# One join fewer on VectorE and score groups at places of their own, in a fused attention, Fourier and feed-forward kernel

## The chip, the cores and the metric

One Trainium2 chip, of which the kernel uses one core. The metric is the device time of one execution in microseconds; the time before is the median of three runs. Engines are named as the profile names them: PE (TensorE matmul), PEld (TensorE weight load), DVE (VectorE), ACT (ScalarE), POOL (GpSimd), SP (SyncE, which issues most DMAs).

## The reference, cut to what matters

```python
# q, k, v: (8, 8, 576, 64) float32; moe_w_ch1 (512, 2048) and moe_w_ch2 (2048, 512) float64
scores = q @ k.transpose(0, 1, 3, 2) / 8 - slopes[:, None, None] * abs(rel)   # per head
scores = where((rel >= 0) & (rel < 128), scores, -1e9)
attn = softmax(scores, axis=-1)
x = (attn @ v).transpose(0, 2, 1, 3).reshape(8, 576, 512)
u = x + real(fft(fft(x, axis=1), axis=2))
un = layer_norm(u)                       # no gain, no bias
out = u + relu(un @ w_ch1) @ w_ch2
```

## The kernel before, in words

The kernel works batch by batch (eight batches `b`), and inside a batch by pairs of heads: `p` counts pairs through the whole program, four to a batch. Every step is a small Python function that is put into a heap with a due time (`put(t, f, ...)`); the heap is emptied in order of the due times, and a step may put followers a little later (`after`). That sets the order in which instructions are written down. A planner then orders the instructions of each engine, from that order as a priority and from its own costs of instructions, and each engine runs its list in order. So a due time moves an instruction roughly, and the planner decides the last detail.

A pair `p` begins at `begin_of(p)`, every 6 units of due time from `p = 4` on (before that every 2.2). Its scores are made in three groups, `scores(p, i)` with i = 0, 1, 2, over the query tiles (1, 0), (3, 2) and (4). For each of the two heads a group's matmuls (line 378) fill a PSUM tile `sp`; VectorE then adds the bias and takes the row minimum in one instruction (line 391, written as `P` and `nb`), ScalarE takes the exponential. For batches from `NF = 2` on, products are made from pairs of fp16 parts: `halves` (line 404 and a VectorE instruction) splits the weights of attention, and `flip` (line 413) transposes them by DMA from the SP queue into `pt`. `values` (lines 445 to 447) multiplies `pt` with V into `pv`. For batches 0 and 1 the same is done in float32 with transposes on TensorE (`turn`, lines 422 and 426).

In the first four pairs, `busy` (line 299) adds three matmuls of 512 columns on constant data after each block of matmuls, 180 in all; their results are not used.

After a batch's four pairs come a Fourier transform (`fourier`), the normalisation (`norm`) and the feed-forward part (`ffn`, lines 699 and 713), which is by far the largest part of TensorE's work, spread in small steps over the due times of the following batch.

The float64 weights are read at the start as 32-bit words, two per value, in 16 chunks for each of two matrices, at due times 0 to 8 and 9 to 18.6. For a chunk, `load` brings 512 KB; `rebias` (line 183, ScalarE) takes the upper word as a float32, makes its absolute value and shifts its exponent by a factor of 2^-112; `join` (lines 188 to 190, VectorE) shifts the result left by three bits, joins the top bits of the lower word, and joins the sign bit of the upper word. `gram` (line 198) squares the chunk on TensorE for a scale, and when all 16 are there `high` and `low` (lines 216 and 219) split the scaled matrix into two fp16 parts, which the feed-forward part reads.

For each batch from 2 on, `batch_scales` also reads q, k and v once more through two small slots (lines 253 and 257), for a scale.

The last loop of the kernel puts the pairs' steps; the line that the change touches there is

```python
        for i in range(3):
            put(t + 2 * i * f + (0 if b < NF + 1 else 1 - 2 * ((3 * p + i) % 2)), scores, p, i)
```

With groups numbered 3p + i, group n stands at 2n units. For batches 3 to 7 the term adds one unit to even numbers and takes one from odd ones, so two groups at a time are due at the same place, every four units. `values` for x = 0 to 5 (head of the pair x // 3, tiles of group x % 3) are due at t + x + 5.66 and don't move.

Of the kernel before, what the change touches and what calls it, by code (L numbers as in the profile page):

```python
# [10 lines left out]
F32 = mybir.dt.float32  # L11
# [3 lines left out]
AF = mybir.ActivationFunctionType  # L15
ALU = mybir.AluOpType
# [6 lines left out]
NF = 2  # L23
# [32 lines left out]
def begin_of(p):  # L56
    return 6 * PACE[0] * p if p < 4 else T1 + 6 * (p - 4)
# [6 lines left out]
def forward_of(b):  # L64
    return transform_of(b) + (START - DFT if b else 11 * PACE[1])
# [11 lines left out]
def attn_fft_ffn_kernel(  # L77
# [16 lines left out]
    V, A, G, T = nc.vector, nc.scalar, nc.gpsimd, nc.tensor  # L94
# [46 lines left out]
    def total(m):  # L141
        sums = ps_d.tile([128, 512], F32, name="pd")[:, 0:m.shape[1]]
        T.matmul(sums, misc[:, 7:8].broadcast_to([128, 128]), m, start=True, stop=True)
        return sums

    def root_inv(dst, src):
        V.tensor_scalar(dst, src, 0.5, 2.0 ** -81, ALU.mult, ALU.max)
        V.tensor_scalar(dst.bitcast(I32), dst.bitcast(I32), 1, 0x3F800000, ALU.logical_shift_right, ALU.bitwise_and)
        V.reciprocal(dst, dst)
# [4 lines left out]
    def put(t, f, *a):  # L154
        heappush(queue, (t, next(order), f, a))
# [8 lines left out]
    def weights(wi, t0, dt, t1, dt1):  # L164
        w, top = ((w1, 2.0 ** 7), (w2, 2.0 ** 14))[wi]
        raws, box = {}, {}
        if wi == 0:
            stages = [hbuf[:, o:o + 1024] for o in range(0, 4096, 1024)]
        else:
            stages = [stage[:, 0:1024], stage[:, 1024:2048], wall[1][:, 0]]  # L170
        ns = len(stages)

        def load(c):
            raws[c] = stages[c % ns]
            nc.sync.dma_start(out=raws[c].bitcast(I32), in_=w[:, c * 512:(c + 1) * 512].bitcast(I32))

        def words(c):
            return (raws[c].bitcast(I32).rearrange("p (a b) -> p a b", b=2),
                    wall[wi][:, 1 + c // 2, c % 2 * 512:c % 2 * 512 + 512])

        def rebias(c):
            raw, dst = words(c)
            A.activation(dst, raw[:, :, 1].bitcast(F32), AF.Abs, scale=2.0 ** -112)

        def join(c):
            raw, dst = words(c)
            bits = dst.bitcast(I32)
            V.tensor_scalar(bits, bits, 3, None, ALU.logical_shift_left)
            V.scalar_tensor_tensor(bits, raw[:, :, 0], 29, bits, ALU.logical_shift_right, ALU.bitwise_or)
            V.scalar_tensor_tensor(bits, raw[:, :, 1], -0x80000000, bits, ALU.bitwise_and, ALU.bitwise_or)  # L190

        def gram(c):
            if c == 0:
                box["gram"] = ps_f.tile([128, 512], F32, name="fp")[:, 0:128]
            upper = words(c)[1].bitcast(BF16).rearrange("p (x e) -> p x e", e=2)[:, :, 1]
            for j in range(4):
                blk = upper[:, j * 128:(j + 1) * 128]
                T.matmul(box["gram"], blk, blk, start=(c == 0 and j == 0), stop=(c == 15 and j == 3))

        def top_of():  # L200
            m1 = small.tile([128, 2], F32, name="wm1", tag="m2")
            V.tensor_reduce(m1[:, 0:1], box["gram"], AX.X, ALU.max)
            box["sums"] = total(m1[:, 0:1])

        s = wsc[:, wi:wi + 1]

        def scale():
            root_inv(s, box["sums"])
            V.tensor_scalar_mul(s, s, top * 2.0 ** -64)
            if wi == 1:  # L210
                V.tensor_tensor(wone, wsc[:, 0:1], wsc[:, 1:2], ALU.mult)
                V.tensor_scalar_mul(wone, wone, 8.0)
                V.reciprocal(wone, wone)

        def high(g):
            A.activation(wf[wi][:, g, 0], wall[wi][:, g + 1], AF.Copy, scale=s)  # L216

        def low(g):
            V.scalar_tensor_tensor(wf[wi][:, g, 1], wall[wi][:, g + 1], s, wf[wi][:, g, 0], ALU.mult, ALU.subtract)

        for c in range(16):
            t = t0 + dt * c
            put(-3 + 0.1 * c if c < ns else t + dt * (1 - ns) - 0.05, load, c)
            put(t, rebias, c)
            put(t + dt - 0.1, join, c)
            put(t + 2 * dt - 0.3, gram, c)
        t = t0 + 17 * dt
        put(t, top_of)
        put(t + 0.3, scale)
        for g in range(8):  # L230
            put(t1 + dt1 * g, high, g)
            put(t1 + dt1 * (g + 0.8), low, g)
# [490 lines left out]
    for p in range(4 * B):  # L723
        b, j = divmod(p, 4)
        t, f = begin_of(p), 1 if b else PACE[0]
        put(t - 7 * f if p else -3.2, load, p)
        if b < NF:
            put(t - 3.8 * f if p else -2, convert, p, 0)
            put(t - 1.2 * f, load_v, p)
            put(t + 4.2 * f, v_max, p)  # L730
        else:
            early = p < 4 * NF + 2
            put(t - (1.3 if early else 6.8), load_v, p)
            for what, x in enumerate((4.6, 3.6, -2 if early else 1.2)):
                put(t - x, convert, p, what)
        for i in range(3):
            put(t + 2 * i * f + (0 if b < NF + 1 else 1 - 2 * ((3 * p + i) % 2)), scores, p, i)
            for e in range(2 if b < NF else 0):
                put(t + (2 * i + e + LB + 0.33) * f, turn, p, i, e)
        for x in range(6):  # L740
            put(t + (x + LC + 0.66) * f, values, p, x % 3, x // 3)
        if b < NF and j == 3:
            put(t + 5 * f, f32_scale, b)
# [5 lines left out]
    for b in range(B):  # L749
        t = begin_of(4 * b)  # L750
# [4 lines left out]
        t = forward_of(b)  # L755
# [88 lines left out]
def program(q, k, v, moe_w_ch1, moe_w_ch2):  # L844
    import numpy as np
    import concourse.bacc as bacc

    B = q.shape[0]
    qa = np.ascontiguousarray(q.transpose(0, 1, 3, 2)[..., query_order()]).reshape(B, 4, 128, NQ)
    ka = np.concatenate([k, k[:, :, :NK - S]], axis=2).transpose(0, 1, 3, 2)  # L850
    ka = np.ascontiguousarray(ka).reshape(B, 4, 128, NK)
    idx = np.array([[min(s + p, S - 1) for s in VSTART] for p in range(128)])
    va = np.ascontiguousarray(v[:, :, idx])
    nf = min(B, NF)
    v0 = np.ones((nf, H, 128, 5, 65), np.float32)
    v0[..., 0:D] = va[:nf]
    w1 = np.ascontiguousarray(moe_w_ch1.reshape(4, 128, 16, 128).transpose(1, 2, 0, 3).reshape(128, -1))
    w2 = np.ascontiguousarray(moe_w_ch2.reshape(16, 128, DM).transpose(1, 0, 2).reshape(128, -1))
    w1, w2 = w1.view(np.int64), w2.view(np.int64)
    rel, slope, tab1, tab2 = tables()  # L860
    nc = bacc.Bacc("TRN2", target_bir_lowering=False, num_devices=1, dynamic_dma_scratch_size=1024)
    arrays, args = {}, []
    for name, a in (("q", qa), ("k", ka), ("v", va), ("v0", v0), ("w1", w1), ("w2", w2), ("rel", rel),
                    ("slope", slope), ("tab1", tab1), ("tab2", tab2)):
        arrays[name + "_dram"] = a
        args.append(nc.dram_tensor(name + "_dram", a.shape, mybir.dt.from_np(a.dtype), kind="ExternalInput").ap())
    rows = B * S
    args.append(nc.dram_tensor("out_dram", (rows, DM), F32, kind="ExternalOutput").ap())
    with tile.TileContext(nc, schedule_with_timeline_sim=True) as tc:
        attn_fft_ffn_kernel(tc, *args)  # L870
    return nc, arrays, B
```

## Time and profile before

| | |
|---|---|
| median of 3 runs | 1132.4 us |
| lowest and highest run | 1125.85, 1135.44 us |
| profiled execution, first to last instruction | 1129.0 us |
| mean granted TensorE clock in it | 0.974 |
| TensorE busy (matmul) | 1064.1 us, 94% |
| VectorE busy | 710.9 us, 63% |
| ScalarE busy | 583.7 us, 52% |

The profiled execution is one of its own; its time is its span, 1129.0 us, with whatever lies outside the first and the last instruction not shown. It is 3.4 us under the median of the runs. The busy shares are means over stages with different limits: the first 110 us hold the weights and the first batch's attention, up to some 340 us only the first batch's feed-forward part can fill TensorE, from there to 930 us attention, Fourier and feed-forward parts of following batches run side by side, and after 930 us only feed-forward work is left.

### The profile page before, as it was taken

Reading aid. Unit: us, or ns where it says so; the run is one execution under the profiler, and the core shown is the slowest. Engines: PE = TensorE matmul, PEld = TensorE weight load, DVE = VectorE, ACT = ScalarE, POOL = GpSimd, SP = SyncE. Lnnn points to the kernel's source line nnn. Section 1 sums busy time; section 2 is a strip of 40 time slices with the busy share of each in tenths; the row PEclk is TensorE's granted clock in tenths of the full one; section 3 lists DMA queues with packets and bytes.
Section 4 is the critical chain, followed back from the end, with each engine's and each line's share of the span. In section 5 each row is a group of like instructions: output and inputs, shape, how many; then the busy total and the mean of one; then the engine's idle time right before and its main releaser. Section 6 shows DMA issues by size and latency. Waiting matters only on the chain.

```text
span 1129.0 us, 23955 instructions
## 1 busy us (share of the span) xinstructions
PE 1064.1 (94%) x9296; PEld 742.2 (66%) x9296; DVE 710.9 (63%) x2081; ACT 583.7 (52%) x1380; POOL 19.6 (2%) x59
## 2 busy tenths in 40 slices
PE   7999989978789989999999989999899989999998
PEld 4667767464475757777667667585758567667665
DVE  6989668725866576768677585869575754362111
ACT  5757889657774465437554474456434631151010
POOL 0000000000000000000000000000000000010000
PEclk9999859999799999999999989999999999999999
DMA  9951647666863335332734243333531240010000
GB/s 368 333 156 41 180 129 189 177 160 163 200 138 106 68 96 110 77 89 65 136 93 86 42 116 75 83 87 85 119 91 32 41 106 1 20 43 24 19 10 20
DMA packets 191506, 117.82 MB, mean 104 GB/s; under 512 B 154400, under 2 KB 164128, under 8 KB 191392
## 3 DMA queue, kind: packets, MB, share of 16 engines
q1 hardware_dynamic: 190816, 114.84, 40.6%
q8 instruction: 73, 1.20, 0.4%
q10 hardware_dynamic: 576, 1.45, 0.3%
q14 instruction: 41, 0.34, 0.1%
HBM read 70.63 MB, written 9.44 MB: 71 GB/s over the span
## 4 chain that ended last, share of the span: by engine, by line
PE 63%; DVE 13%; DMA 10%; ACT 9%; issue 3%; SPq 1%; POOL 0%; DVEq 0%; ACTq 0%
PE fp L713 26%; PE fp L699 23%; DMA pt<-P 4%; PE sp L378 4%; PE fp L299 3%; PE pd L555 2%; DVE P L391 2%; ACT wall L257 2%; DMA wall<-k_dram 2%; DMA wall<-q_dram 2%; DMA wall<-v_dram 2%; PE pv L440 1%; ACT P L158 1%; DVE P L158 1%; ACT wall L216 1%
## 5 line engine op out<-in xcount | busy, mean ns | idle before, releaser
L713 PE MATMUL fp<-wall,hbuf 128*128 128x512 f16 x1728 | 393.0, 382 | 3.3 <-ACT P L404 1.8
L699 PEld LDWEIGHTS <-wall 128*128 128x128 f16 x3840 | 342.9, 99 | 67.3 <-issue 21.5
L699 PE MATMUL fp<-uT,wall 128*128 128x256 f16 x3072 | 361.8, 275 | 17.3 <-DVE hbuf L158 11.1
L713 PEld LDWEIGHTS <-hbuf 128*128 128x128 f16 x1728 | 163.3, 98 | 189.1 <-issue 7.2
L704 ACT ACTIVATE hbuf<-fp 128x512 f16<-128x512 f32 x144 | 84.9, 590 | 208.6 <-PE fp L699 208.2
L158 DVE SCALAR_TENSOR_TENSOR hbuf<-fp,hbuf 128x512 f16<-128x512 f32 x144 | 98.8, 687 | 137.5 <-ACT hbuf L704 136.7
L158 ACT ACTIVATE P<-P,nb 128x256 f32<-128x256 f32 x320 | 139.9, 479 | 61.6 <-DVE nb L391 60.8
L391 DVE CUSTOM_DVE_ANT_0 P<-sp,rg,nsl 128x256 f32<-128x256 f32 x240 | 97.3, 449 | 37.5 <-DMA pt<-P 19.5
L158 DVE SCALAR_TENSOR_TENSOR P<-P 128x256 f16<-128x256 f32 x240 | 87.8, 389 | 33.6 <-ACT P L404 32.6
L404 ACT ACTIVATE P<-P 128x256 f16<-128x256 f32 x240 | 85.7, 385 | 40.7 <-DMA pt<-P 24.3
L378 PE MATMUL sp<-kk,qq 64*128 64x256 f16 (+5 forms) x880 | 88.3, 295 | 11.5 <-DVE nb L391 6.0
L257 ACT ACTIVATE wall<-wall 128x512 f32<-128x512 f32 (+2 forms) x90 | 54.6, 607 | 48.8 <-DMA wall<-v_dram 18.5
L445 PE MATMUL pv<-vhs,pt 128*128 128x65 f16 x432 | 56.7, 196 | 15.0 <-DMA pt<-P 13.9
L445 PEld LDWEIGHTS <-pt 128*128 128x128 f16 x432 | 41.3, 98 | 24.5 <-DMA pt<-P 14.9
L446 PE MATMUL pv<-vl,pt 128*128 128x64 f16 x432 | 56.4, 194 | 0.0
L447 PE MATMUL pv<-vhs,pt 128*128 128x65 f16 x432 | 56.1, 195 | 0.0
L158 DVE SCALAR_TENSOR_TENSOR X<-fp,misc,X 128x512 f32<-128x512 f32 x32 | 23.8, 743 | 46.3 <-PE fp L713 44.6
L699 PE MATMUL fp<-wall,wall 128*128 128x128 f16 x768 | 48.4, 229 | 4.0 <-DVE pm L515 2.3
L299 PE MATMUL fp<-tab_sb 128*128 128x512 f16 x180 | 48.0, 396 | 1.1 <-DMA tab_sb<-tab_dram 1.1
L378 PEld LDWEIGHTS <-qq 64*128 64x128 f16 (+1 forms) x720 | 33.2, 100 | 21.4 <-issue 17.6
L446 PEld LDWEIGHTS <-pt 128*128 128x128 f16 x432 | 40.9, 99 | 6.8
L447 PEld LDWEIGHTS <-pt 128*128 128x128 f16 x432 | 41.2, 99 | 0.8
(146 smaller groups left out, 1195.1 us busy)
## 6 DMA issues: line engine op xcount, KB each, us to landing
qr<-q_dram SPq DMA_DIRECT2D x32, 304.0 KB, 3.1
hbuf<-w_dram SPq DMA_DIRECT2D x16, 512.0 KB, 6.8
out_dram<-X SPq DMA_DIRECT2D x32, 256.0 KB, 2.3
wall<-v_dram SPq DMA_DIRECT2D x30, 256.0 KB, 2.8
vr<-v_dram SPq DMA_DIRECT2D x24, 320.0 KB, 3.2
kr<-k_dram SPq DMA_DIRECT2D x24, 289.0 KB, 3.4
wall<-q_dram SPq DMA_DIRECT2D x24, 256.0 KB, 2.9
wall<-k_dram SPq DMA_DIRECT2D x24, 256.0 KB, 2.9
```

Source lines behind the costliest of these rows:

```text
L158: put(now[0] + dt, lambda: f(*a, **kw))
L257: A.activation(t, t, AF.Square, accum_out=box["mx"][:, i, c:c + 1])
L299: T.matmul(spin, trig[:, 0:128], trig[:, 0:512], start=True, stop=True)
L378: T.matmul(sp[e][:m, col:col + n], qq[h, c0:c0 + m], keys(kk[h], ti), start=(x == 0), stop=(x == len(prods) - 1))
L391: V.tensor_tensor_reduce(pt[:m, 0:n], sp[e][:m, col:col + n], tab[:m, pc:pc + n], mul, 3.0e38, ALU.add, ALU.min, nb[:m, ti:ti + 1])
L404: A.activation(hi, P32, AF.Copy, scale=2.0 ** 14)
L445: T.matmul(pv[:, ti], ph, vh[:, e, vc], start=first, stop=False)
L446: T.matmul(pv[:, ti, 0:D], ph, vl[:, e, vc], start=False, stop=False)
L447: T.matmul(pv[:, ti], pl, vh[:, e, vc], start=False, stop=last)
L699: T.matmul(fp[:, i * n:(i + 1) * n], w1_ap(e, c, f0 + i), uT[:, j, c, 0:n], start=(c == 0 and p == 0), stop=(c == 3 and p == 2))
L704: A.activation(ht[:, 0], fp, AF.Relu)
L713: T.matmul(op, hh[f][:, a, i * 128:(i + 1) * 128], w2_ap(e, f), start=(f == 0 and p == 0), stop=(f == 15 and p == 2))
```

## The change

`rebias` uses ScalarE's function with a slope for negative inputs in place of the absolute value. A positive upper word is scaled by 2^-112 as before; a negative one is scaled by 2^-112 and by the slope 2^32, which adds 32 to its exponent field. The shift by three bits in `join` carries that bit of the exponent to the place of the sign, and shifts the old sign bit out. So `join` no longer has its third instruction, which put the sign in. Nothing else in the weights' path is changed.

In the last loop, the scores of group n are due at 2n units in all batches: in batches 3 to 7 the even groups come one unit earlier than before and the odd ones one unit later.

```diff
         def rebias(c):
             raw, dst = words(c)
-            A.activation(dst, raw[:, :, 1].bitcast(F32), AF.Abs, scale=2.0 ** -112)
+            A.activation(dst, raw[:, :, 1].bitcast(F32), AF.Prelu, scale=2.0 ** -112, alpha=2.0 ** 32)
...
             V.scalar_tensor_tensor(bits, raw[:, :, 0], 29, bits, ALU.logical_shift_right, ALU.bitwise_or)
-            V.scalar_tensor_tensor(bits, raw[:, :, 1], -0x80000000, bits, ALU.bitwise_and, ALU.bitwise_or)
...
         for i in range(3):
-            put(t + 2 * i * f + (0 if b < NF + 1 else 1 - 2 * ((3 * p + i) % 2)), scores, p, i)
+            put(t + 2 * i * f, scores, p, i)
```

## Rows read from the trace of the kernel before

**Rows 1.** The page's head: span; busy time, share and instructions of each engine.

```profile
span 1129.0 us, 23955 instructions
...
PE 1064.1 (94%) x9296; PEld 742.2 (66%) x9296; DVE 710.9 (63%) x2081; ACT 583.7 (52%) x1380; POOL 19.6 (2%) x59
```

**Rows 2.** Busy time by stage; columns: length, engines, granted clock, DMA share, GB/s.

```profile
10.00:30.00 20.00, 19.22 (x110) 10.72 (x111) 18.68 (x56) 15.64 (x36) 0.00 (x0) 1.00 1.03 403
30.00:70.00 40.00, 40.00 (x259) 25.06 (x259) 39.97 (x116) 27.93 (x59) 0.11 (x1) 1.00 0.86 291
70.00:110.00 40.00, 38.84 (x308) 28.74 (x306) 31.87 (x100) 27.38 (x52) 0.00 (x0) 1.00 0.21 61
110.00:340.00 230.00, 196.94 (x1596) 142.13 (x1596) 152.68 (x482) 171.67 (x447) 4.96 (x16) 0.90 0.66 166
340.00:930.00 590.00, 570.39 (x5487) 398.99 (x5486) 406.75 (x1212) 300.50 (x712) 10.64 (x27) 0.99 0.39 85
```

**Rows 3.** Groups by line, 10 to 80 us: busy and mean ns; idle before.

```profile
L299 PE MATMUL fp<-tab_sb 128*128 128x512 f16 x150 | 40.2, 400 | 1.1 <-DMA tab_sb<-tab_dram 1.1
...
L190 DVE SCALAR_TENSOR_TENSOR wall<-hbuf,wall 128x512 int32<-128x512 int32 x16 | 10.8, 682 | 0.0
...
L183 ACT ACTIVATE wall<-hbuf 128x512 f32<-128x512 f32 x15 | 9.8, 670 | 0.0
```

**Rows 4.** Line 190 alone, 10 to 80 us: length, DVE busy, clock, DMA, GB/s.

```profile
10.00:80.00 70.00, 21.58 (x32) 1.00 0.82 290
```

**Rows 5.** The chain of waits, 0 to 60 us: start, length, what.

```profile
46.67 1.94 PE fp L299 x9
...
48.67 2.01 PE pv L440 x18
```

**Rows 6.** DMA, 10 to 80 us: rate in 40 slices, and the total.

```profile
GB/s 400 421 414 397 382 402 398 414 398 404 404 404 412 314 376 242 192 337 353 344 365 320 428 346 260 337 260 84 159 276 321 331 122 246 44 255 0 0 0 37
DMA packets 6937, 20.30 MB, mean 290 GB/s; under 512 B 727, under 2 KB 1751, under 8 KB 6930
```

**Rows 7.** Busy time in slices of 10 us, columns as in rows 2.

```profile
100.00:110.00 10.00, 8.84 (x80) 7.13 (x78) 10.00 (x34) 8.51 (x18) 0.00 (x0) 1.00 0.17 58
110.00:120.00 10.00, 8.16 (x51) 6.40 (x51) 8.91 (x35) 7.57 (x19) 0.10 (x1) 0.83 0.56 170
...
140.00:150.00 10.00, 10.00 (x36) 7.32 (x34) 7.00 (x27) 5.79 (x18) 0.87 (x3) 0.50 0.20 56
150.00:160.00 10.00, 7.08 (x32) 6.30 (x30) 7.78 (x42) 8.79 (x18) 0.69 (x1) 0.50 0.42 103
```

**Rows 8.** Who waited for whom, 340 to 930 us: total, times, longest.

```profile
ACT P L404 <- DMA pt<-P: 20.4, 20, 3.2
...
DVE P L391 <- DMA pt<-P: 11.4, 8, 2.6
...
PE pv L445 <- DMA pt<-P: 10.5, 3, 4.4
```

**Rows 9.** Timeline around two gaps: start, length, engine, line; in brackets idle before.

```profile
412.37 0.48 DVE L391 CUSTOM_DVE_ANT_0 P<-sp,rg,nsl 128x256 f32<-128x256 f32 x1
...
422.01 3.81 SPq L413 DMA_TRANSPOSE pt<-P  x3
...
424.53 0.24 PE L445 MATMUL pv<-vhs,pt 128*128 128x65 f16 x1 [4.36 <-DMA pt<-P]
...
665.24 0.23 PE L445 MATMUL pv<-vhs,pt 128*128 128x65 f16 x1 [4.24 <-DMA pt<-P]
```

**Rows 10.** Busy time in slices of 4 us, columns as in rows 2.

```profile
424.00:428.00 4.00, 3.47 (x36) 3.47 (x37) 4.00 (x14) 0.31 (x1) 0.00 (x0) 0.57 0.40 82
...
664.00:668.00 4.00, 2.76 (x30) 2.76 (x31) 4.00 (x12) 1.03 (x3) 0.00 (x0) 0.50 0.50 101
668.00:672.00 4.00, 4.00 (x54) 4.00 (x53) 3.52 (x18) 2.20 (x6) 0.69 (x1) 0.71 0.58 140
```

**Rows 11.** Groups by line, the whole span: ScalarE's table loads.

```profile
L119 ACT ACT_TABLE_LOAD x1 | 1.3, 1283 | 2.6 <-issue 2.6
```

## The prediction

> **What bounds the kernel now.** I read the head of the page first [rows 1]: TensorE is busy for 1064.1 of 1129.0 us, so at most 65 us of the span are gaps in its stream, and everything else a change can give back must come from work taken off TensorE or from its clock. Then the stages [rows 2]. Between 10 and 110 us TensorE is busy for 19.22 + 40.00 + 38.84 = 98.1 of 100 us. VectorE is full there too: 18.68 of 20 and 39.97 of 40 us up to 70 us. From 110 to 340 us TensorE has 230 - 196.94 = 33.1 us of gaps and a mean granted clock of 0.90, which costs 0.10 x 196.94 = 19.7 us more: this is the loosest stage. From 340 to 930 us it has 590 - 570.39 = 19.6 us of gaps at a clock of 0.99 (some 5.7 us).
>
> A busy share alone doesn't prove that TensorE is the limit in the first stage, since two engines are full there. The Trainium skill speaks against reading it so: its page "Trainium Kernel Development and Optimization", section Performance Expectations, calls matmul busy time a bad metric because matmuls are pipelined; by it VectorE could be the limit of 10 to 70 us, and this is my first rival below.
>
> So I looked at single pieces. The chain of waits has nine spin matmuls in 1.94 us [rows 5], 0.216 us each, while one matmul of that form takes 400 ns from its start to its end [rows 3]: they overlap, and the next block (line 440, 18 matmuls in 2.01 us) follows within 0.06 us [rows 5]. TensorE streams without holes from 30 to 70 us. A good part of it is the spin: 150 matmuls up to 80 us [rows 3], at 0.216 us 32 us. They are not in the change's reach.
>
> **The change part by part.**
>
> The third join: 32 instructions of 682 ns each, 21.58 us of VectorE between 10 and 80 us [rows 3, 4]. All of it is gone. What hides it today is the TensorE stream above: if TensorE is the limit, VectorE's 21.6 us become idle time until about 80 us and the stage keeps its length. What can be gained is what TensorE waits for behind the weights: the split of the first matrix (line 219) lies in between the first folds of the Fourier transform, and between 100 and 120 us VectorE is full (10.00 and 8.91 of 10 us) while TensorE has gaps of 1.16 and 1.84 us and a clock of 0.83, 0.17 x 8.16 = 1.4 us [rows 7]. If the joins end earlier and pull the split ahead of the folds, these 1.16 + 1.84 + 1.4 = 4.4 us can go. I take 3 of them. The lower end of this part is 0; its upper end, when VectorE is the limit, is 21.6 us, cut by the transfers: 20.30 MB come in between 10 and 80 us, at up to some 400 GB/s [rows 6], so they need 51 us, and 70 - 51 = 19 us is all that the stage could shrink.
>
> The slope in place of the absolute value: 32 instructions on ScalarE, 670 ns for the old function [rows 3]. The trace has no instruction with a slope. The nearest row is the old one, of the same shape and operands, so I count nothing; the other end is a table load around each, which is a rival below. ScalarE is busy for 27.93 of 40 us in that stretch [rows 2], so a tenth more per instruction (2 us in all) would lie beside other work.
>
> Loads of weights: the third join was the last reader of a chunk's buffer; now the second is, so a buffer comes free 0.68 us earlier and the next 512 KB are issued earlier, ahead of the loads of q, k and v on the same SP queue. The DMA engines are full until about 30 us (share 1.03 [rows 2]), so what the weights gain there the other loads lose. I count 0; a load of the second pair that comes a whole transfer late would cost 512 KB / 400 GB/s = 1.3 us.
>
> The scores' places: no instruction is added or taken. In batches 3 to 7 there are 5 x 4 x 3 = 60 groups, 30 come one unit earlier and 30 one unit later. A unit is 5.0 us here: the two like gaps at 424.53 and 665.24 us [rows 9] are 240.7 us apart, and their place recurs after two batches, 48 units. With each group move its row minima on VectorE, its exponentials and splits on ScalarE and its transposes on the SP queue (past other transposes, loads, and stores of results); loads, conversions and `values` stay. From the due times, the lead of a group's scores over its `values` was 4.66, 5.66 and 2.66 units in an even pair and 6.66, 3.66 and 4.66 in an odd one; it becomes 5.66, 4.66 and 3.66 in all. The shortest lead grows by 5 us, and the longest shrinks.
>
> What it can give: TensorE waits three times, 10.5 us in all, for transposed weights [rows 8]. The two large waits are of one kind [rows 9]: row minima of the pair of groups at 412.37 us, their first transpose issued only at 422.01, landed before the matmul at 424.53. Those 9.6 us from minimum to issue are long because four groups' worth of splits queue behind the batch boundary's work on VectorE, which is full in both slices behind the waits, 4.00 of 4 us [rows 10]. After each gap the clock falls: 0.43 x 3.47 + 0.50 x 2.76 + 0.29 x 4.00 = 4.0 us [rows 10]. Together 14.5 us hang on this one pattern. Pairs of groups also fill the nine `P` buffers at once: ScalarE waited 20.4 us and VectorE 11.4 us for a transpose to free one [rows 8]; these lie beside TensorE's work and count only where they delay something else. I take half of 14.5, about 7 us, since a wait that ends earlier meets the same full VectorE at the boundary, and the second group of an even pair now has the lead of 4.66 units with which the first one waited. Ends of this part: all gaps and clock of the stage, 19.6 + 5.7 = 25 us gained; or as many new waits as there are now, 14.5 us lost.
>
> The sum: 3 + 7 = 10 us. On the profiled execution 1129.0 - 10 = 1119.0 us; the median of the runs is 3.4 us above that execution's span, so 1132.4 - 10 = 1122.4 us.
>
> **The rivals.**
>
> 1. VectorE is the limit of the first stage. For it: VectorE's 39.97 of 40 us [rows 2]. Against: TensorE's stream has no holes there either [rows 5]. Gain 19 us instead of 3, with 7 from the scores: 1132.4 - 26 = 1106 us.
>
> 2. Nothing comes through: the weights' share is hidden by the spin and by TensorE's own work, and the waits for transposes come back at other groups of the same boundaries. For it: the boundary's load on VectorE isn't changed. 1132.4 - 2 = 1130 us.
>
> 3. Slower: the planner's new order leaves a second hole in TensorE's stream between 110 and 340 us, and the clock goes with it. There is one now: from 140 to 160 us TensorE runs at 0.50, 1.2 instead of 2.4 GHz, after gaps, and in 150 to 160 it idles for 2.9 us [rows 7]. Such a hole costs 0.5 x (10.00 + 7.08) + 2.9 = 11.5 us. It decides from one such hole on, without the scores' gain: 1132.4 + 11.5 = 1144 us. For it: VectorE's work before 110 us gets another order, and the first feed-forward part is the only filler after it. Against: less work on VectorE rather makes holes smaller.
>
> 4. The slope isn't in the table set that is loaded. There is one load in the span, 1283 ns [rows 11], and all functions so far run on it. If the slope needed another set, each of 32 instructions would cost a load there and, where an exponential or copy follows, one back: 32 to 64 loads x 1.283 = 41 to 82 us of ScalarE, which has 12 of 40 us free in the stage [rows 2]: at least 1132.4 + 41 - 20 = 1153 us, and about 1190 at the upper end. The Trainium skill's page "ScalarE: Activation LUTs", section Table sets: the hidden batching unit, says that cheap functions are in every set and names relu, abs, copy and identity, but not this one; it gives some 2.66 us for a switch, and by that the price would be twice mine. That one load serves exponential, absolute value, square, relu and copies agrees with it.
>
> **How the numbers follow.** The forecast (3 from the weights, 7 from the scores, each within some 5 us): 0.50, and 1112 to 1132 us by itself. Rival 1: 0.16. Rival 2: 0.20. Rival 3: 0.11. Rival 4: 0.03. A measurement of this kernel tells about 1%, 11.3 us, from no change: faster is under 1121.1, slower over 1143.7 us. Faster: rival 1 and just over half of the forecast, 0.16 + 0.26 = 0.42. Slower: rivals 3 and 4, 0.14. The same: 0.44. The range goes from 1104, below rival 1's 1106, to 1138: it leaves out rivals 3 and 4 and some 0.05 of larger gains, under 0.2 in all.
>
> **What would show it.** Right: line 190 gone with 32 instructions less on VectorE; TensorE's first 70 us as full as before and the first fold of batch 0 within 3 us of its old place; gaps and clock of 100 to 120 us smaller; no wait of over 2 us for `pt` near 424 and 665 us, and less waiting for `P` buffers. Rival 1 shows as the first fold 10 us or more earlier. Wrong: a second table load; a longer stretch at a clock of 0.50 before 340 us; waits for `pt` at the same boundaries with other groups. What would upset the forecast most is the order between 110 and 340 us, where 53 us of gaps and clock lie and of which I only count 4.4.

## The result, and the profile after

The changed kernel takes 1118.42 us (median of 7 runs, 1114.22 to 1126.92) against 1132.4 us; the ratio is 0.9899 with a 95% interval of 0.9855 to 0.9942. That is 14 us where 10 were forecast, and inside the range. The profiled execution spans 1116.6 us, 12.4 us less than before. Where some executions of a kernel run longer at a lower mean clock, the ratios below are taken from the faster ones alone.

The busy times of the page's head, and the busy time by stage (columns as in rows 2):

```profile
PE 1068.9 (96%) x9296; PEld 739.7 (66%) x9296; DVE 695.4 (62%) x2049; ACT 582.0 (52%) x1380; POOL 19.8 (2%) x59
```

```profile
10.00:30.00 20.00, 19.62 (x122) 11.74 (x123) 15.38 (x52) 16.23 (x36) 0.00 (x0) 1.00 1.03 404
30.00:70.00 40.00, 40.00 (x285) 26.87 (x283) 32.90 (x104) 28.81 (x62) 0.11 (x1) 1.00 0.82 304
70.00:110.00 40.00, 37.15 (x286) 27.75 (x284) 29.84 (x99) 28.86 (x56) 0.10 (x1) 0.95 0.23 65
110.00:340.00 230.00, 199.41 (x1593) 143.91 (x1591) 148.52 (x471) 169.29 (x437) 4.55 (x15) 0.87 0.64 163
340.00:930.00 590.00, 586.55 (x5607) 404.09 (x5608) 411.28 (x1216) 300.84 (x719) 11.16 (x27) 1.00 0.39 86
...
100.00:110.00 10.00, 7.16 (x39) 4.78 (x38) 10.00 (x34) 8.41 (x18) 0.10 (x1) 0.81 0.25 69
110.00:120.00 10.00, 10.00 (x43) 7.33 (x42) 5.08 (x23) 5.80 (x17) 0.00 (x0) 0.50 0.48 145
```

Read against [rows 1, 2]: VectorE has 32 instructions less and is less busy in the first stage (15.38 and 32.90 us where 18.68 and 39.97 stood), while TensorE is busy for as long as it was, 40.00 of 40 us. Yet in these 40 us it ran 285 matmuls in place of 259: a busy TensorE was not a TensorE at its limit. Three landmarks show what came of that, in the kernel before and then in the changed one: the spin, the small memset that opens a batch's transform (its first start is called the first fold of batch 0 below), and the first half of the feed-forward part (duration in ns, lowest, median and highest; first and last start):

```profile
L299 PE MATMUL fp<-tab_sb x180: 377/379/635, 9.9 to 93.0; 128*128 128x512 f16 x180
L503 DVE MEMSET X<- x8: 485/485/485, 99.7 to 953.3; 1x512 f32 x8
L699 PE MATMUL fp<-uT,wall x3072: 268/273/422, 160.8 to 1083.2; 128*128 128x256 f16 x192
...
L298 PE MATMUL fp<-tab_sb x180: 377/379/634, 10.1 to 87.0; 128*128 128x512 f16 x180
L502 DVE MEMSET X<- x8: 485/485/485, 94.7 to 940.9; 1x512 f32 x8
L698 PE MATMUL fp<-uT,wall x3072: 269/273/421, 167.6 to 1070.8; 128*128 128x256 f16 x192
```

The spin ends 6 us sooner and the transform opens 5 us sooner, so part of the 21.6 us did come through; but the first feed-forward matmul comes 6.8 us later.

The stages from 70 to 340 us and from 340 to 930 us go opposite ways. From 340 to 930 us TensorE's gaps fell from 19.6 to 3.45 us and its clock is 1.00: some 20 us gained. Between 70 and 340 us it got worse by some 7 us, an estimate from the rows by stage: gaps and clock cost 1.16 + 33.1 + 0.10 x 196.94 = 53.9 us before, and 2.85 + 30.6 + 0.05 x 37.15 + 0.13 x 199.41 = 61.2 us now. The last two rows by stage answer to the first two of [rows 7]: TensorE has 2.84 us of gaps between 100 and 110 us, and then runs at 0.50, the lower of its two levels (1.2 GHz), for the whole next slice.

TensorE's longest remaining wait between 340 and 930 us (total, times, longest):

```profile
PE pv L444 <- DMA pt<-P: 2.0, 1, 2.0
```

The three waits for transposed weights, 10.5 us [rows 8], have become one of 2.0, at 341.8 us and not at a batch boundary; nothing is left at the two places of [rows 9]. ScalarE's waits for a free `P` buffer fell from 20.4 to 2.4 us in that stage and VectorE's from 11.4 to 1.0. There is still one table load; its row is that of [rows 11], word for word.

### The profile page after: what moved, and what is told of

It is laid out like the page before. It is cut to its first block, busy times and chain, and to the rows that moved or that the text cites. A ratio compares the mean times of both kernels' runs of the same rounds, so it can differ in the third digit from the quotient of the medians.

```text
span 1116.6 us, 23914 instructions
## 1 busy us (share of the span) xinstructions
PE 1068.9 (96%) x9296; PEld 739.7 (66%) x9296; DVE 695.4 (62%) x2049; ACT 582.0 (52%) x1380; POOL 19.8 (2%) x59
## 4 chain that ended last, share of the span: by engine, by line
PE 75%; DMA 10%; DVE 7%; ACT 6%; issue 1%; SPq 1%; ACTq 0%; DVEq 0%
PE fp L698 30%; PE fp L712 28%; PE sp L377 4%; DMA wall<-q_dram 3%; PE pd L554 2%; PE fp L298 2%; DMA wall<-v_dram 2%; DMA wall<-k_dram 2%; ACT wall L256 2%; PE pv L439 2%; DMA pt<-P 1%; PE pd L588 1%; ACT P L158 1%; PE pv L444 1%; DVE P L390 1%
## 5 line engine op out<-in xcount | busy, mean ns | idle before, releaser
L698 PE MATMUL fp<-uT,wall 128*128 128x256 f16 x3072 | 366.3, 276 | 14.6 <-DVE hbuf L158 7.4
L444 PE MATMUL pv<-vhs,pt 128*128 128x65 f16 x432 | 55.0, 195 | 2.4 <-DMA pt<-P 2.0
L446 PE MATMUL pv<-vhs,pt 128*128 128x65 f16 x432 | 55.3, 194 | 0.0
L444 PEld LDWEIGHTS <-pt 128*128 128x128 f16 x432 | 41.0, 98 | 12.4 <-issue 3.4
L439 PEld LDWEIGHTS pv<-vr,pt 128*128 128x128 f32 x288 | 43.1, 225 | 3.9 <-issue 1.0
L698 PE MATMUL fp<-wall,wall 128*128 128x128 f16 x768 | 45.4, 219 | 0.1
L445 PEld LDWEIGHTS <-pt 128*128 128x128 f16 x432 | 40.7, 99 | 6.4
```

What stands on the lines that cost most here:

```text
L439: T.matmul(pv[:, ti], pt[:, col:col + 128], ops[p][2][:, e, vc], start=first, stop=last)
L444: T.matmul(pv[:, ti], ph, vh[:, e, vc], start=first, stop=False)
L445: T.matmul(pv[:, ti, 0:D], ph, vl[:, e, vc], start=False, stop=False)
L698: T.matmul(fp[:, i * n:(i + 1) * n], w1_ap(e, c, f0 + i), uT[:, j, c, 0:n], start=(c == 0 and p == 0), stop=(c == 3 and p == 2))
```

## The experiments

Theory S: the gain comes from the scores' places, and TensorE with its spin hides what is taken off VectorE. Rival W: the join carries it. Rival P: any edit lets the planner shuffle the instructions, and the gain is luck of the order. All ratios are to the kernel before, run on the same chip in the same hours.

**Each part alone.**

```diff
 # weights alone: before, with
+            A.activation(dst, raw[:, :, 1].bitcast(F32), AF.Prelu, scale=2.0 ** -112, alpha=2.0 ** 32)
-            V.scalar_tensor_tensor(bits, raw[:, :, 1], -0x80000000, bits, ALU.bitwise_and, ALU.bitwise_or)
 # scores alone: before, with
+            put(t + 2 * i * f, scores, p, i)
```

Expected of the weights alone: 

> Only the weights' part: slope on ScalarE, no third join; the scores stay in pairs. Theory S (the gain comes from the scores' places; TensorE hides the weights' part): 1127 to 1137 us, the waits for transposed weights between 340 and 930 us are still there, 15 us or more of gaps in that stage. Rival W (the 21.6 us taken off VectorE carry the gain): 1113 to 1122 us. Rival P (any edit lets the planner shuffle the order and the gain is luck of it): anywhere from 1115 to 1145, with the gaps at new places.

Expected of the scores alone: 

> Only the scores' part: each group at its own place, the third join stays. Theory S: 1110 to 1121 us, gaps of TensorE between 340 and 930 us under 8 us, the stage before 340 us as in the kernel before. Rival W: 1128 to 1135 us. Rival P: anywhere from 1115 to 1145.

The weights' part alone is slower: 1138.37 us, ratio 1.0061 (1.0027 to 1.0095). The scores' part alone is 1114.46 us, ratio 0.9839 (0.9793 to 0.9884). W falls. Theory S holds for the scores; the weights alone are just past its upper end of 1137 us. The stages of the weights alone, and then of the scores alone:

```profile
110.00:120.00 10.00, 10.00 (x44) 7.22 (x44) 4.81 (x22) 6.58 (x19) 0.00 (x0) 0.50 0.50 143
...
110.00:340.00 230.00, 196.16 (x1537) 141.02 (x1537) 142.02 (x445) 167.35 (x433) 4.41 (x15) 0.85 0.64 160
340.00:930.00 590.00, 570.26 (x5478) 398.91 (x5476) 410.75 (x1232) 302.94 (x717) 10.67 (x27) 0.99 0.39 85
```

```profile
110.00:120.00 10.00, 8.16 (x51) 6.55 (x51) 8.84 (x36) 7.14 (x18) 0.10 (x1) 0.83 0.54 168
...
110.00:340.00 230.00, 196.97 (x1592) 142.51 (x1592) 150.28 (x477) 172.18 (x449) 4.95 (x16) 0.90 0.65 165
340.00:930.00 590.00, 589.24 (x5676) 407.60 (x5674) 415.68 (x1227) 300.67 (x717) 11.28 (x27) 1.00 0.39 86
```

The two parts act in different stages. The weights alone keep the 19.7 us of gaps after 340 us, at the old kinds of places (4.36 and 4.25 us for `pt` at 435.7 and 677.2 us), and have the slice at half clock; their first feed-forward matmul comes at 168.1 us, against 161.9 with the scores alone. The scores alone have the stages from 70 to 340 us of the kernel before, almost digit for digit, and 0.76 us of gaps after 340 us.

**The slope by itself.** The changed kernel, with a third instruction in `join` that joins nothing; every engine's list is the same, in the same order, as with the scores alone.

```diff
+            V.scalar_tensor_tensor(bits, raw[:, :, 1], 0, bits, ALU.bitwise_and, ALU.bitwise_or)
```

Expected: 

> The changed kernel with the slope on ScalarE, and a third VectorE instruction in the join again that joins nothing (the sign's mask is zero), so every engine has the same list of instructions in the same order as in the run with the scores' part alone; only ScalarE's function differs. If the slope costs nothing: 1110 to 1119 us and ScalarE's 32 instructions at 0.67 us. If the slope itself is dear (a table load, a slower function), the weights' part loses here as in the run with it alone: 1120 us or more.

1116.16 us, ratio 0.9845 (0.9800 to 0.9890), and ScalarE's instruction takes what it took:

```profile
L183 ACT ACTIVATE wall<-hbuf 128x512 f32<-128x512 f32 x15 | 9.9, 670 | 0.6 <-DMA hbuf<-w_dram 0.6
```

The slope is free: 670 ns, as for the absolute value [rows 3]. The Trainium skill's page "ScalarE activation tables: per-element evaluation and per-set limits", section What a function is on this engine, says that with the same operands an instruction costs the same whichever table is read; this pair of rows agrees. So what the weights' part loses comes from the missing join. That it does so through the order that the planner then makes is argued: no run takes the join away and keeps the order.

**Pairs or lead?** The changed kernel with the pairs in the other phase, and with all groups one unit later, each still alone:

```diff
 # other phase
+            put(t + 2 * i * f + (0 if b < NF + 1 else 2 * ((3 * p + i) % 2) - 1), scores, p, i)
 # one unit later
+            put(t + 2 * i * f + (0 if b < NF + 1 else 1), scores, p, i)
```

Expected of the other phase: 

> The changed kernel, but the groups of batches 3 to 7 in pairs of the other phase: odd groups one unit later, even ones one unit earlier. Leads over their values are 6.66, 3.66 and 4.66 units in an even pair and 4.66, 5.66 and 2.66 in an odd one: the same three sets as in the kernel before, with even and odd swapped. If pairing itself makes the waits (two groups' buffers at once), they come back: 1128 to 1135 us and 15 us or more of gaps from 340 to 930 us. If the kernel before had only an unlucky phase against the batch boundary, this one stays under 1122 us.

Expected of one unit later: 

> The changed kernel with every group of batches 3 to 7 one unit (5 us) later, each still at a place of its own: leads of 4.66, 3.66 and 2.66 units, the shortest as in the kernel before. If the lead decides, the waits for transposed weights come back (10 us or more between 340 and 930 us, 1126 to 1134 us). If spreading the groups decides, the time stays within 5 us of the changed kernel, with gaps of that stage under 8 us.

Other phase: 1125.34 us, 0.9930 (0.9895 to 0.9964). One unit later: 1128.88 us, 0.9971 (0.9941 to 1.0002). Their stage from 340 to 930 us, in this order, each with TensorE's waits for `pt` in it (total, times, longest):

```profile
340.00:930.00 590.00, 580.32 (x5601) 406.41 (x5600) 408.53 (x1213) 301.69 (x710) 12.10 (x27) 1.00 0.39 84
...
PE pv L444 <- DMA pt<-P: 2.4, 2, 2.1
```

```profile
340.00:930.00 590.00, 576.79 (x5511) 400.66 (x5509) 409.14 (x1216) 299.37 (x715) 10.79 (x27) 0.99 0.41 86
...
PE pv L444 <- DMA pt<-P: 6.0, 3, 2.6
```

Pairs in the other phase bring back 9.7 us of gaps, of which 2.4 are for `pt` and 7.2 for the feed-forward part's evictions on VectorE; ScalarE waits 13.5 us for `P` buffers again. Groups alone but 5 us later have 13.2 us of gaps, and TensorE waits 6.0 us for `pt` (2.59 and 2.51 us at 427.6 and 665.4 us, the old boundaries) and 7.1 us for such evictions, although ScalarE's waits for `P` buffers are down to 2.4 us. So neither half of my expectations holds alone. Pairing makes the waits for buffers, 13.5 us against 2.4. The waits for `pt` go with the lead, but not with it alone: the shortest lead is 2.66 units in both phases, in the odd pairs here and in the even pairs in the kernel before, and leaves 2.4 us of such waits here against 10.5 [rows 8]. The waits for evictions come in both.

In time, groups that are late lose most of the gain: one unit later is not told from the kernel before. What pairing alone costs is not shown: the interval of the other phase overlaps that of the changed kernel, and its profiled execution, the fastest of ten, took as long as the changed kernel's (1118.97 and 1118.42 us). So the change needs groups that are early enough; that they need places of their own is shown for the waits for buffers, not for the time.

**The spin and the clock.** Theory C came out of the first runs: with the join gone the spin ends earlier (its last matmul starts at 87.0 us against 92.9 with the scores alone), TensorE runs dry between 100 and 108 us, where VectorE is full, and is then granted half its clock. Three kernels change the spin: to six pairs (`p < 6`) in the changed kernel, and to one matmul in place of three (`SPIN = 1`) in the changed kernel and in the one with the scores alone.

Expected of six pairs: 

> The changed kernel with the spin matmuls also in the fifth and sixth pair (270 in all, some 19 us more of TensorE's work, until past 110 us). Theory C (the weights' part loses because TensorE runs dry at 100 to 108 us, earlier spin gone, and is granted half its clock until some 123 us): the clock stays at 1.00 through 120 us, and first feed-forward matmul comes no later than 163 us; the time lies between 1108 and 1120 us as the spin's own work is weighed against it. Rival Q (it is VectorE's queue, not the clock, that delays the transform): the clock stays up, and the first feed-forward matmul comes as late as before or later, with 1120 to 1135 us.

Expected of one spin, changed kernel: 

> The changed kernel with one spin matmul in place of three (60 in all; some 26 us of TensorE's work less before 90 us). If TensorE with its spin is what hides the freed VectorE time, the first fold of batch 0 (94.7 us in the changed kernel) comes 10 us or more earlier here. If something else (VectorE's own chain, the transfers) paces it, it moves by under 4 us. The time as a whole may be worse for a lower clock: 1105 to 1135 us.

Expected of one spin, scores alone: 

> The scores' part alone (third join still there) with one spin matmul in place of three. VectorE was full from 10 to 72 us. If TensorE alone was the limit, the first fold (some 100 us) comes 10 us or more earlier as well; if VectorE was as near to being the limit, it comes only some 5 us earlier, and the difference to the changed kernel with one spin is what the third join is worth once the spin doesn't hide it, 5 to 15 us in the place of the fold.

With six pairs the clock is 1.00 from 100 to 130 us, and the first feed-forward matmul comes at 180.4 us, 12.8 us later than in the changed kernel; 1132.51 us, 0.9991 (0.9973 to 1.0010). Theory C's forecast (163 us, and 1108 to 1120 us) failed. Rival Q's came true, but the run doesn't settle it: the spin's own 19 us (an estimate, 90 matmuls at 0.216 us) stand in TensorE's queue among the matmuls of the transform, the last of them at 140.6 us. What it shows is that a clock bought this way costs more than it gives.

With one spin, the first fold of batch 0 comes at 90.4 us in the changed kernel (94.7 with three) and at 93.4 with the scores alone (99.5). Taking some 26 us of TensorE's work away moves it by 4.3 and 6.1 us. So the spin hid only a part; with it gone the clock falls instead (0.67 from 70 to 100 us in the changed kernel), and the freed join is worth 3.0 us in the place of the fold, against 4.8 with the spin. The expectations of a fold 10 us earlier, and of a join worth 5 us or more without the spin, were wrong: TensorE, VectorE and the clock are near to each other as limits here. The times were 1124.3 us for the changed kernel (0.9919, 0.9889 to 0.9949), and for the scores alone four executions in two groups, 1113.35 and 1113.85 us at a mean clock of 0.966 and 0.962 (0.9827, 0.9777 to 0.9877), 1137.25 and 1139.0 at 0.939 and 0.942. So with one spin, too, the kernel without the third join is the slower one, and here the intervals stand apart.

**The place of the split.** Four kernels move the weights' due times:

```diff
 # split two units later: in the changed kernel, and with the scores alone
+    weights(0, 0.0, 0.5, 11.0, 0.8)
 # chunks faster and split earlier, changed kernel
+    weights(0, 0.0, 0.4, 7.5, 0.6)
 # chunks a little faster, scores alone
+    weights(0, 0.0, 0.45, 9.0, 0.8)
```

In the first two, the reads for batch 2's scale land in the buffer of the last eighth of the first matrix before it is split, so that eighth isn't the matrix's; the instructions are the same in number and shape.

Split later, changed kernel: 

> The changed kernel with the split of the first weight matrix due two units later (11 in place of 9), out of the stretch at 90 to 110 us in which VectorE is full. If VectorE's queue there starves TensorE and lets its clock fall to half from 107 to 123 us (theory C), the clock in 100 to 130 us rises from 0.72 to 0.85 or more, and the time comes to 1108 to 1115 us, level with the scores' part alone. If the loss is only the planner's order (rival P), the time moves without relation to that clock.

Split later, scores alone: 

> The scores' part alone, third join kept, with the same later split. A control for the run before: here the clock in 100 to 130 us is 0.94 already, so theory C expects little, 1108 to 1118 us; rival P expects a spread like that of any other reordering, 1105 to 1130 us.

Split earlier, changed kernel: 

> The changed kernel with the first matrix' chunks due faster (0.4 in place of 0.5 units each) and its split from 7.5 in place of 9 units, 0.6 apart, so that the split can use the VectorE time that the third join left idle between 60 and 80 us. If that idle time can be used: VectorE under 9 of 10 us between 100 and 110 us, the clock of 100 to 130 us at 0.85 or more, 1103 to 1114 us, the best so far. If TensorE's order (the gram of all 16 chunks) sets the place of the split, nothing moves: 1115 to 1124 us.

Chunks a little faster, scores alone: 

> The scores' part alone, third join kept, first matrix' chunks due every 0.45 in place of 0.5 units: the same work in another order (thousands of places differ on TensorE). It measures what a reordering of the first 110 us is worth by itself: under theory C it follows the clock of 100 to 170 us, at 1110 to 1118 us when that is as in the run with the scores' part alone. Rival P: it is off by 5 us or more at the same clock.

Later split, changed kernel: 1112.44 us, 0.9838 (0.9799 to 0.9876), a clock of 0.89 from 100 to 130 us. These are theory C's numbers, but not its mechanism: VectorE is still full from 100 to 110 us, and TensorE idles there for 4.92 us, longer than the 2.84 us of the changed kernel. The control: 1123.7 us, 0.9926 (0.9901 to 0.9951), 9 us above the scores alone for the same edit, where theory C had at most 1118 us; its profile has a clock of 0.83 there, and 5.0 us of gaps after 340 us. Chunks a little faster, the third join kept: 1118.37 us, 0.9892 (0.9846 to 0.9937). This one is the most telling. A slice of it, and then 100 to 170 us with the scores alone and in this run:

```profile
120.00:130.00 10.00, 10.00 (x41) 7.43 (x40) 1.95 (x8) 4.88 (x15) 0.00 (x0) 0.50 0.38 121
...
100.00:170.00 70.00, 62.08 (x424) 48.96 (x422) 50.13 (x184) 57.90 (x147) 1.86 (x7) 0.78 0.48 132
...
100.00:170.00 70.00, 62.43 (x403) 47.97 (x402) 46.75 (x180) 57.98 (x154) 2.42 (x7) 0.78 0.54 142
```

The slice at half clock comes with the full join, from nothing but another order of the same work; the first feed-forward matmul comes at 168.4 us and the time is 1118 us, both as in the changed kernel. So the stretch at half clock belongs to the order of the instructions around 110 us, not to the join as such. Nor is the clock what makes this run longer than the scores alone: over 100 to 170 us it is 0.78 in both, and the median is 3.9 us higher, past the 1118 us that theory C had for that case, though the two intervals overlap. With the control, whose interval stands apart, a reordering of the early stage alone is worth 4 to 9 us in this kernel. The loss of the weights' part is of the same size: that much of rival P stands.

Split earlier: 1108.54 us, 0.9823 (0.9767 to 0.9879), the best median of all. VectorE's idle time between 60 and 80 us is put to use: it is busy for 14.79 us there against 9.34, and for 8.83 of 10 us from 100 to 110, as expected. That the gain comes from it is not shown, since a reordering alone is worth nearly as much; and the interval overlaps those of the scores alone and of the changed kernel. The clock failed the expectation in the profiled execution (0.72 from 100 to 130 us), but that one is the slowest of the four: 1118.32 us at a mean clock of 0.969, where the others took 1106.69 to 1109.0 at 0.978 to 0.985.

## Why the prediction was right, and where it was not

The time and the direction were right; of the two terms one was too small and the other had the wrong sign. That 10 us were forecast and 14 measured is luck in the size: one term was 11 us too small, the other 7 to 10 us too large, and the errors nearly cancelled.

**The scores' term was 7 us and measured 18** (0.9839 of 1134.4 us, the median before in that session). The pattern was the forecast one: the waits of [rows 9] and the slow clock behind them [rows 10] are gone, and so are the waits for buffers. The size was off in the step where half of 14.5 us was taken because "a wait that ends earlier meets the same full VectorE". It didn't: nearly all gaps of the stage went, not only those for `pt`, and the upper end, 25 us, was nearer. The reading of the waiting group was off as well. At 424.53 us six matmuls wait, on two blocks of keys, so it is the third group of an even pair that waits, with a lead of 2.66 units and not 4.66, and its row minima are those before the row in [rows 9], 11.4 us ahead of the transposes:

```profile
410.61 0.47 DVE L391 CUSTOM_DVE_ANT_0 P<-sp,rg,nsl 128x256 f32<-128x256 f32 x1
```

The change gave this lead one unit more, 3.66, just where the wait stood. The waits for `P` buffers, which I set beside the path, sat in the queues of ScalarE and VectorE that also evict the feed-forward part. That they delayed it is not shown: with all groups one unit later ScalarE's were down to 2.4 us, and TensorE still waited 7.1 us for evictions.

**The weights' term was a gain of 3 us and measured a loss of 4 to 7**: 1.0061 alone (4 us by the medians, 7 by the ratio), and 0.9899 against 0.9839 on top of the scores, where the intervals overlap. Two steps failed. The first is that "the stage keeps its length" behind a full TensorE: the last spin matmul came 6 us sooner and the first fold 5.0 us (94.7 against 99.7, where I had allowed 3), at the same busy time. The second is that "the lower end of this part is 0". The stretch from 100 to 120 us cost 4.4 us in gaps and clock, of which I expected 3 back; by the same sum it now costs 2.84 + 0.19 x 7.16 + 0.50 x 10.00 = 9.2 us. The split was pulled ahead by 3 us (82.0 against 85.2 us) and the fold by 5, so both still met at 100 us, now without spin beside them. Of my own signs, the fold's place and the smaller gaps and clock of that stretch failed, and a sign of being wrong came: a longer stretch at half clock before 340 us. It is rival 3's mechanism, smaller than its price of 11.5 us and as a companion of the forecast instead of a rival to it.

How much of the loss is the clock's is open. The mean granted clock over all executions was 0.9628 with the weights alone against 0.9708 before, and 0.9703 in the changed kernel against 0.9773 with the scores alone. 0.8% of 1132 us is 9 us, 0.7% of 1114 is 8: by this estimate the clock accounts for all of the loss, and the 1 to 2 us left over are less than the intervals resolve. But kernels at an equal clock differ by more: the two with the later split took 1112.4 and 1123.7 us at 0.9755 and 0.9747. What is shown is that the slope is free, that the loss comes with the missing join, and that another order alone makes the same stretch at half clock and the same late feed-forward part. Why the planner's order after the missing join does so is open: the later split helped in one kernel and hurt in the other.

**Rival 1** (VectorE as the limit) fell as a gain, since the weights alone were slower, but not as a mechanism: 5 us of the 21.6 reached the first fold, half of the 10 that were its sign. The one-spin runs add that the engines were close. **Rival 2** fell with the gaps after 340 us. **Rival 4** fell: one table load.

## What to carry to other kernels

Time taken off an engine that shares a full stage with another need not be a gain, even where it moves the next work ahead: here 21.6 us less for VectorE brought the first fold 5 us forward and the first feed-forward matmul 7 us back. An engine that is busy without a hole can still get the same work done sooner, so the places of landmarks (a last spin, a first fold) say more than its busy share. A wait of TensorE at a boundary is best read back to its first instruction: ten microseconds between the row minima and the issue of the transpose pointed to the lead and the burst, and the run one unit later bears the lead out. Where a planner orders the instructions, a part's worth should be measured alone and against another order of the same work before it is believed.

## What the runs showed of the hardware that was not expected

Executions of one and the same kernel differ in time and in granted clock together: before, 29 executions in one session went from 1123.53 us at a mean granted clock of 0.980 to 1139.58 us at 0.965. That is 16 us for 0.015, about one per cent of time for each per cent of clock. An estimate, a straight line through the 29 pairs, has 9 us for 0.01 and carries 73% of their variance; whether the clock or the wait behind it comes first, these numbers don't say.

TensorE's busy time can be the same to the hundredth, 40.00 of 40 us, while the same work is done 5 to 6 us sooner.
